# Starting the couples of 64-row products one phase earlier, and a convolution four units later

## The chip, the cores and the metric

The kernel runs on one core of a Trainium2 chip. The metric is device time in microseconds (us). Of this core, five engines matter: TensorE (PE in the profile; its weight loads are listed as PEld), VectorE (DVE), ScalarE (ACT), GpSimd (POOL, almost unused) and SyncE (SP), which issues the transfers. Each engine takes its instructions in the order in which the program wrote them; they wait for each other by semaphores.

## The reference, cut to what matters

```python
# 1. a causal convolution of 7 taps along the sequence; the taps are a softmax, one set per head of 24 channels
w = softmax(weight)                              # 8 heads x 7 taps
x = einsum('hk,bskhg->bshg', w, unfold(pad(x)))  # x: 2 x 4096 x 192
# 2. a feed-forward layer, 192 -> 2048 -> 192
h = x @ w_in
g = where(h >= 1, h, where(h <= -1, 0, (h + 1)**2 / 4))
x = g @ w_out
# 3. a second one with other weights
h = x @ w2_in
out = (h * sigmoid(1.702 * h)) @ w2_out
```

All is in float32. The 8192 tokens are cut into 16 blocks of 512; channels lie on partitions, tokens along the free axis.

## The kernel before, in words

**Units, phases, steps.** The work of one layer on one block is a phase: (1, i) is the first feed-forward layer on block i, (2, i) the second. A phase has 16 units, one for each 128 of the 2048 hidden channels. A list written out by hand sets the order: units 0 to 31 are phases (1, 0) and (1, 1), four units of one and four of the other in turn; units 32 to 47 are (1, 2); 48 to 79 are (2, 0) and (2, 1) in turn; from 80 on, whole phases alternate, (1, 3), (2, 2), (1, 4), (2, 3) and so on to unit 511. Unit numbers serve as steps, too: a plan (`at(step, op)`) says which other work is issued beside which unit.

**One unit.** `gemm1` makes 128 hidden channels of 512 tokens in a PSUM bank `h`. `act_a` applies the activation: for layer 1 a relu and a square on ACT (L272, L273) and a max/min on DVE (L274) that reads `h` again; for layer 2 one gelu on ACT (L276). `act_b` splits the result in two float32r parts: `ghi` by a cast on ACT (L73), `glo` by a subtraction on DVE (L74). `gemm2` multiplies both with the output weights into two accumulator banks; it runs four units (`LAG`) behind `gemm1`. Inputs are split as well: `xah` and `xal` are the parts of a block's first 128 channels, `xb` and `xc` hold the two parts of its 64 last channels.

**Two ways to issue a unit's products.** Up to unit 47 (`WHOLE` = 3 * NF, NF = 16) a unit is ten products over 128 rows, five in `gemm1` and five in `gemm2`. From there on `both(u, v)` issues two units at once: 19 products of `gemm1` u, u+1 and `gemm2` v, v+1 (v = u - 4) that use rows 0 to 63, and 19 that use rows 64 to 127, in turn, so that the two halves of the array run side by side. The lower list begins with `gemm1` and ends with `gemm2`, the upper one the other way round. `act_a` and `act_b` of a couple are issued for both units after it, and behind them the work planned beside its two steps. The first couple, u = `WHOLE`, is still issued with whole products.

**Beside the units** stand three kinds of work. (1) Weights are turned from 64-bit words to two float32r parts in four pieces at steps s to s+3 (`weight_ops`): `begin` (ACT L117, DVE L118), `join` (DVE L122), `high_part` (ACT copy L127, which reads what `join` wrote), `low_part` (DVE L131, L132). For the second layer s = 31 + 9f // 4. (2) `finish` reads an ended phase's accumulators; for layer 1 that is L372, a split into `xah`/`xal`, an add (L374) and a split into `xb`. (3) Convolutions: block 0 and 1 are done at the start; `conv_at(j)` plans those of blocks 2j and 2j+1. For block 2j, seven taps on DVE (L152, L153) make the first 128 channels `cva`, `put_a` splits them into `xah`/`xal`; seven more make the 64 last channels of both blocks `cvb`, and `put_b` splits those. One of these 16 pieces stands at each step from `first - 22` on, where `first` is the unit at which block 2j's phase begins (32 for j = 1, then 112, 176 and so on for j = 2 to 7).

Of the kernel before, what the change touches and what calls it, by code (L numbers as in the profile page):

```python
# [20 lines left out]
def kernel(  # L21
# [24 lines left out]
    NF, _, WC = w1.shape  # L46
    DB = D - P
    B = P // DB
# [1 line left out]
    H = P // 2  # L50
    LAG = 4
    CH = 4
    WHOLE = 3 * NF

    const = ctx.enter_context(tc.tile_pool(name="const", bufs=1))
    wpool = ctx.enter_context(tc.tile_pool(name="wpool", bufs=1))
# [15 lines left out]
    def split(src, hi, lo):  # L72
        nc.scalar.copy(hi, src)  # L73
        nc.vector.tensor_sub(lo, src, f32(hi))  # L74
# [64 lines left out]
    def new_xs():  # L139
        return [xs_p.tile([P, T], F32R, tag=t, name=t) for t in ("xah", "xal", "xb", "xc")]  # L140
# [7 lines left out]
    def conv_taps(part, t, c):  # L148
        def tap(k):
            w, x = taps[:, part, k : k + 1], t[:, k : k + T]  # L150
            if k == 0:
                return lambda: nc.vector.tensor_scalar_mul(c, x, w)  # L152
            return lambda: nc.vector.scalar_tensor_tensor(c, x, w, c, op0=ALU.mult, op1=ALU.add)  # L153

        return [tap(k) for k in range(K)]
# [18 lines left out]
    def put_a(i, c):  # L174
        split(c, *x1[i][:2])

    def swap_halves(dst, src):
        nc.sync.dma_start(f32(dst[0:DB]), f32(src[DB:P]))
        nc.sync.dma_start(f32(dst[DB:P]), f32(src[0:DB]))

    def put_b(i, c):

        b, halved = i % B, phases.index((1, i)) * NF >= WHOLE
        t = x1[i][2 + (b if halved else 0)]
        hi, lo = (t[0:DB], t[DB:P]) if b == 0 else (t[DB:P], t[0:DB])
        split(c[b * DB : (b + 1) * DB], hi, lo)
        if halved:
            swap_halves(x1[i][3 - b], t)

    def conv_ops(j):  # L190

        ta, tb = xt[0, B * j], xt[1, j]
        ca = cv_p.tile([P, T], F32, tag="cva", name="cva")
        cb = cv_p.tile([P, T], F32, tag="cvb", name="cvb", bufs=1)
        x1[B * j] = new_xs()
        ops = conv_taps(0, ta, ca) + [lambda: put_a(B * j, ca)]
        ops += conv_taps(1, tb, cb) + [lambda: put_b(B * j, cb)]
        st = {}

        def begin():  # L200
            st["c"] = cv_p.tile([P, T], F32, tag="cva", name="cva")
            x1[B * j + 1] = new_xs()
            st["ops"] = conv_taps(0, xt[0, B * j + 1], st["c"])
            put_b(B * j + 1, cb)

        ops.append(begin)
        ops += [lambda: st["ops"].pop(0)() for _ in range(K)] + [lambda: put_a(B * j + 1, st["c"])]
        return ops
# [28 lines left out]
    def gemm1(u):  # L237

        ah, al, b, _ = x_of(u)
        h = hid[u] = bank(HID + u % 4, f"h{u}")  # L240
        hi, lo = hidden_w(u)
        prods = [
            (lo[:, 0:P], ah),
            (hi[:, 0:P], al),
            (hi[:, 0:P], ah),
            (lo[:, P : 2 * P], b),
            (hi[:, P : 2 * P], b),
        ]
        for j, (w, r) in enumerate(prods):
            nc.tensor.matmul(h, w, r, start=j == 0, stop=j == len(prods) - 1)  # L250
# [28 lines left out]
    def act_b(u):  # L279
        a = act.pop(u)  # L280
        hi = g_p.tile([P, T], F32R, tag="ghi", name="ghi")
        lo = g_p.tile([P, T], F32R, tag="glo", name="glo")
        split(a, hi, lo)
        halves[u] = (hi, lo)
# [81 lines left out]
    def finish(p, step):  # L366
        n, i = phases[p]
        acc_a, acc_b = accs.pop(p)
        if n == 1:
# [6 lines left out]
            def put():  # L376
                split(s[0:DB], b[0:DB], b[DB:P])
                if phases.index((2, i)) * NF >= WHOLE:
                    swap_halves(c, b)
# [13 lines left out]
    def at(step, op):  # L393
        plan.setdefault(max(step, 0), []).append(op)
# [14 lines left out]
    def fetch_x(*which):  # L409
        for part, i in which:  # L410
            xt[part, i] = x_load(part, i)

    def conv_at(j):
        first, second = (unit_at[phases.index((1, B * j + k)), 0] for k in range(B))
        ops = []
        at(first - 30, lambda: fetch_x((0, B * j), (1, j), (0, B * j + 1)))
        at(first - 22, lambda: ops.extend(conv_ops(j)))
        for k in range(2 * (K + 1)):
            at(first - 22 + k, lambda: ops.pop(0)())
        for k in range(K + 2):  # L420
            at(second - 16 + k, lambda: ops.pop(0)())

    with tc.manual_schedule():
# [14 lines left out]
        ca = cv_p.tile([P, T], F32, tag="cva", name="cva")  # L438
# [31 lines left out]
        for j in range(1, NBLK // B):  # L470
            conv_at(j)
# [5 lines left out]
        def finish_if_last(u, step):  # L477
            if 0 <= u < len(units) and units[u][1] == NF - 1:
                finish(units[u][0], step)


        for step in range(WHOLE):
            gemm1(step)
# [8 lines left out]

        act_b(WHOLE - 1)
        for u in range(WHOLE, len(units) + LAG + 4, 2):
            v = u - LAG
            if u == WHOLE:
                finish_if_last(v - 1, u)
# [71 lines left out]
```

## Time and profile before

| what | us |
|---|---|
| three runs: median (lowest to highest) | 1138.95 (1138.84 to 1139.42) |
| the profiled execution's own time | 1139.2 |
| its span in the trace | 1137.4 |
| PE busy in the span | 1127.7 (99%) |
| ACT busy | 823.3 (72%) |
| DVE busy | 713.7 (63%) |

Busy time is time with at least one instruction of the engine in flight. The products of PE overlap: one lasts about 386 ns, and the next starts 227 ns after it (or at the same time in the other half of the array). So PE's share alone says little; where PE waits, the trace shows it as a gap in brackets with the engine that ended it. Averages over the span also mix the first 130 us, in which all weights are converted, with the rest, in which no weights are.

### The profile page before, as it was taken

How to read it: one execution, taken by the hardware profiler on the slowest of the kernel's cores; microseconds unless marked ns; L12 is line 12 of the kernel's file. 1: busy time of each engine (PE TensorE's matmuls, PEld its weight loads, DVE VectorE, ACT ScalarE, POOL GpSimd, SP SyncE). 2: the span in 40 equal slices, each digit the busy share in tenths (PEclk: the TensorE clock that was granted, in tenths of full speed). 3: DMA queues.
4: the chain of work that ended last, by engine and by line, in shares of the span. 5: the costliest groups of instructions: out<-in, count | busy, mean ns of one | idle time of the engine just before them, and what ended most of it. 6: DMA issues, size and time to landing. Idle time of an engine off the chain costs nothing.

```text
span 1137.4 us, 22818 instructions
## 1 busy us (share of the span) xinstructions
PE 1127.7 (99%) x9324; PEld 927.1 (82%) x9324; DVE 713.7 (63%) x1152; ACT 823.3 (72%) x1467; POOL 7.1 (1%) x13
## 2 busy tenths in 40 slices
PE   9999999999999999999999999999999999999998
PEld 5878888888888888888888888888888888888886
DVE  7998765675557756476564756647566575655432
ACT  7989875867758677686776768677586776868654
POOL 2000000000000000000000000000000000000000
PEclk9999999999999999999999999999999999999999
DMA  5321320100001000010000100010000100000000
GB/s 176 124 65 43 123 75 11 57 10 25 10 11 43 18 17 10 11 43 20 15 20 13 31 20 15 20 43 1 20 15 20 44 1 20 15 20 15 11 15 14
DMA packets 16535, 36.40 MB, mean 32 GB/s; under 512 B 2480, under 2 KB 2480, under 8 KB 16432
## 3 DMA queue, kind: packets, MB, share of 16 engines
q1 hardware_dynamic: 16432, 34.96, 10.5%
q8 instruction: 73, 1.20, 0.5%
q14 instruction: 30, 0.25, 0.1%
HBM read 21.05 MB, written 6.29 MB: 24 GB/s over the span
## 4 chain that ended last, share of the span: by engine, by line
PE 93%; DVE 3%; ACT 2%; issue 1%; DMA 0%; SPq 0%
PE acc L358 46%; PE h L358 42%; PE h L250 3%; DVE glo L74 1%; DVE a L274 1%; PE acc L309 1%; PE acc L312 1%; PE acc L310 1%; PE acc L311 1%; PE ca_ps L170 1%; PE acc L313 1%; DVE wd L122 0%; DVE cva L153 0%; DMA raw<-in_w_dram 0%; ACT a L273 0%
## 5 line engine op out<-in xcount | busy, mean ns | idle before, releaser
L358 PE MATMUL acc<-ghi,wt 64*128 64x512 f32 x2772 | 835.4, 386 | 0.0
L358 PE MATMUL h<-xah,wt 64*128 64x512 f32 x1848 | 714.0, 386 | 0.0
L358 PE MATMUL acc<-glo,wt 64*128 64x512 f32 x1848 | 678.2, 386 | 0.0
L358 PEld LDWEIGHTS acc<-ghi,wt 64*128 64x128 f32 x2772 | 468.9, 184 | 53.9 <-ACT ghi L73 0.3
L74 DVE TENSOR_TENSOR glo<-a,ghi 128x512 fp32r<-128x512 f32 x512 | 341.5, 688 | 232.8 <-ACT ghi L73 223.5
L358 PEld LDWEIGHTS acc<-glo,wt 64*128 64x128 f32 x1848 | 340.4, 184 | 36.5 <-DVE glo L74 0.8
L358 PEld LDWEIGHTS h<-xah,wt 64*128 64x128 f32 x1848 | 340.4, 184 | 36.1 <-issue 0.4
L358 PE MATMUL h<-xal,wt 64*128 64x512 f32 x924 | 357.0, 386 | 0.0
L73 ACT CAST ghi<-a 128x512 fp32r<-128x512 f32 x512 | 301.7, 615 | 26.2 <-DVE a L274 25.7
L274 DVE SCALAR_TENSOR_TENSOR a<-h,a 128x512 f32<-128x512 f32 x256 | 176.9, 691 | 159.7 <-ACT a L273 159.4
L276 ACT ACTIVATE a<-h 128x512 f32<-128x512 f32 x256 | 150.8, 596 | 153.8 <-PE h L358 145.9
L358 PE MATMUL h<-xb,wt 64*128 64x512 f32 x693 | 231.0, 386 | 0.0
L358 PE MATMUL h<-xc,wt 64*128 64x512 f32 x693 | 230.8, 386 | 0.0
L272 ACT ACTIVATE a<-h 128x512 f32<-128x512 f32 x256 | 151.0, 590 | 53.0 <-PE h L358 52.2
L358 PEld LDWEIGHTS h<-xal,wt 64*128 64x128 f32 x924 | 170.2, 184 | 17.8
L273 ACT ACTIVATE a<-a 128x512 f32<-128x512 f32 x256 | 161.8, 632 | 8.2
L358 PEld LDWEIGHTS h<-xc,wt 64*128 64x128 f32 x693 | 127.7, 184 | 17.9
L358 PEld LDWEIGHTS h<-xb,wt 64*128 64x128 f32 x693 | 127.5, 184 | 9.0
L153 DVE SCALAR_TENSOR_TENSOR cva<-xt,taps,cva 128x512 f32<-128x512 f32 x90 | 67.3, 748 | 1.3
L250 PE MATMUL h<-xah,wt 128*128 128x512 f32 x100 | 40.5, 405 | 2.6 <-DVE wt L131 2.6
L153 DVE SCALAR_TENSOR_TENSOR cvb<-xt,taps,cvb 128x512 f32<-128x512 f32 x42 | 31.4, 747 | 0.4
L250 PE MATMUL h<-xb,wt 128*128 128x512 f32 x100 | 30.9, 391 | 0.5 <-DVE xb L74 0.5
(65 smaller groups left out, 488.2 us busy)
## 6 DMA issues: line engine op xcount, KB each, us to landing
raw<-in_w_dram SPq DMA_DIRECT2D x32, 448.0 KB, 3.4
xc<-xb SPq DMA_DIRECT2D x44, 128.0 KB, 2.2
xt<-in_xa_dram SPq DMA_DIRECT2D x16, 259.0 KB, 3.6
out_dram<-o SPq DMA_DIRECT2D x16, 256.0 KB, 2.0
xt<-in_xb_dram SPq DMA_DIRECT2D x8, 259.0 KB, 3.4
out_dram<-o SPq DMA_DIRECT2D x16, 128.0 KB, 2.2
xb<-xc SPq DMA_DIRECT2D x14, 128.0 KB, 2.2
taps<-in_taps_dram SPq DMA_DIRECT2D x1, 7.0 KB, 1.6
```

What stands on the lines that cost most here:

```text
L73: nc.scalar.copy(hi, src)
L74: nc.vector.tensor_sub(lo, src, f32(hi))
L153: return lambda: nc.vector.scalar_tensor_tensor(c, x, w, c, op0=ALU.mult, op1=ALU.add)
L170: return lambda: nc.tensor.matmul(c, d[:, k], t[:, k : k + T], start=k == 0, stop=k == K - 1)
L250: nc.tensor.matmul(h, w, r, start=j == 0, stop=j == len(prods) - 1)
L272: nc.scalar.activation(a, h, AF.Relu, bias=0.5, scale=0.5)
L273: nc.scalar.activation(a, a, AF.Square)
L274: nc.vector.scalar_tensor_tensor(a, h, 1.0, a, op0=ALU.max, op1=ALU.min)
L276: nc.scalar.activation(a, h, AF.Gelu_apprx_sigmoid)
L309: nc.tensor.matmul(acc_a, wl, hi, start=first, stop=False)
L310: nc.tensor.matmul(acc_a, wh, hi, start=False, stop=False)
L358: mm = nc.tensor.matmul(banks[n], w, r, start=n in fresh, stop=ends.get(n) == k)
```

## The change

`WHOLE` becomes 2 * NF: units 34 to 49 (phase (1, 2) but for its first two units, and the two behind it), eight couples, are now issued as 64-row products, and the couple with whole products is 32, 33 instead of 48, 49. As a consequence block 2's 64 last channels are also swapped into `xc` (two more transfers). In `conv_ops` the seven taps and the split of the 64 last channels come ahead of those of the first 128. In `conv_at` these 16 pieces begin at `first - 18`; the pieces of the second block stay at `second - 16`. This holds for every j.

```diff
@@ -50,7 +50,7 @@
     CH = 4
-    WHOLE = 3 * NF
+    WHOLE = 2 * NF
 
@@ -193,8 +193,8 @@
         x1[B * j] = new_xs()
-        ops = conv_taps(0, ta, ca) + [lambda: put_a(B * j, ca)]
-        ops += conv_taps(1, tb, cb) + [lambda: put_b(B * j, cb)]
+        ops = conv_taps(1, tb, cb) + [lambda: put_b(B * j, cb)]
+        ops += conv_taps(0, ta, ca) + [lambda: put_a(B * j, ca)]
         st = {}
@@ -414,9 +414,9 @@
         at(first - 30, lambda: fetch_x((0, B * j), (1, j), (0, B * j + 1)))
-        at(first - 22, lambda: ops.extend(conv_ops(j)))
+        at(first - 18, lambda: ops.extend(conv_ops(j)))
         for k in range(2 * (K + 1)):
-            at(first - 22 + k, lambda: ops.pop(0)())
+            at(first - 18 + k, lambda: ops.pop(0)())
```

On ACT around unit 36 this stood before: casts, the weight copy (L127), the next weights' `begin` (L117) and one unit's activation after the other (`h36` is unit 36's bank; the number after a name tells buffers apart).

```order
L73 CAST ghi_1059<-a_1027 128x512
L127 CAST wt2_89<-wd_1017 128x448
L117 ACTIVATE wa_1069<-raw_994 128x448
L272 ACTIVATE a_1079<-h36_1073 128x512
L273 ACTIVATE a_1079<-a_1079 128x512
L73 CAST ghi_1083<-a_1055 128x512
L372 COPY s_1098<-acc3_1_417 64x512
```

And this stands there now:

```order
L272 ACTIVATE a_1151<-h36_1109 128x512
L273 ACTIVATE a_1151<-a_1151 128x512
L272 ACTIVATE a_1155<-h37_1110 128x512
L273 ACTIVATE a_1155<-a_1155 128x512
L73 CAST ghi_1159<-a_1151 128x512
L73 CAST ghi_1163<-a_1155 128x512
L127 CAST wt2_89<-wd_1104 128x448
L117 ACTIVATE wa_1172<-raw_1096 128x448
L73 CAST xb_1087<-s_1089 64x512
L272 ACTIVATE a_1226<-h38_1182 128x512
```

Both units' casts stand directly ahead of the weight copy, and the next couple's activation stands behind it. On DVE at the same place, before:

```order
L122 SCALAR_TENSOR_TENSOR wd_1017<-wa_1016,wd_1017 128x448
L74 TENSOR_TENSOR xb_987<-s_989,xb_987 64x512
L274 SCALAR_TENSOR_TENSOR a_1055<-h35_1049,a_1055 128x512
L74 TENSOR_TENSOR glo_1060<-a_1027,ghi_1059 128x512
L118 TENSOR_SCALAR wd_1070<-raw_994 128x448
L274 SCALAR_TENSOR_TENSOR a_1079<-h36_1073,a_1079 128x512
```

And now:

```order
L274 SCALAR_TENSOR_TENSOR a_1151<-h36_1109,a_1151 128x512
L274 SCALAR_TENSOR_TENSOR a_1155<-h37_1110,a_1155 128x512
L74 TENSOR_TENSOR glo_1160<-a_1151,ghi_1159 128x512
L74 TENSOR_TENSOR glo_1164<-a_1155,ghi_1163 128x512
L131 TENSOR_TENSOR wt2_89<-wd_1023,wt2_89 128x384
L132 TENSOR_TENSOR wt2_89<-wd_1023,wt2_89 128x64
L122 SCALAR_TENSOR_TENSOR wd_1104<-wa_1103,wd_1104 128x448
```

The `join` (L122) whose result the ACT copy reads stood ahead of unit 35's max/min (copy of `wd_1017`); now it stands behind both subtractions of its couple (copy of `wd_1104`).

On DVE just ahead of unit 112, where block 4 begins, before: the last tap and the split of the 64 last channels, then three couples' subtractions.

```order
L153 SCALAR_TENSOR_TENSOR cvb_2724<-xt_2479,taps_85,cvb_2724 128x512
L74 TENSOR_TENSOR xb_2727<-cvb_2724,xb_2727 64x512
L74 TENSOR_TENSOR glo_3211<-a_3206,ghi_3210 128x512
L74 TENSOR_TENSOR glo_3215<-a_3208,ghi_3214 128x512
L74 TENSOR_TENSOR glo_3267<-a_3262,ghi_3266 128x512
L74 TENSOR_TENSOR glo_3271<-a_3264,ghi_3270 128x512
L74 TENSOR_TENSOR glo_3323<-a_3318,ghi_3322 128x512
L74 TENSOR_TENSOR glo_3327<-a_3320,ghi_3326 128x512
L274 SCALAR_TENSOR_TENSOR a_3374<-h112_3330,a_3374 128x512
```

Now the last tap and the split of the first 128 channels stand one couple's subtractions ahead of it:

```order
L153 SCALAR_TENSOR_TENSOR cva_3019<-xt_2653,taps_85,cva_3019 128x512
L74 TENSOR_TENSOR xal_3022<-cva_3019,xah_3021 128x512
L74 TENSOR_TENSOR glo_3499<-a_3494,ghi_3498 128x512
L74 TENSOR_TENSOR glo_3503<-a_3496,ghi_3502 128x512
L274 SCALAR_TENSOR_TENSOR a_3550<-h112_3506,a_3550 128x512
```

The last of the 16 pieces moved from couple 104 to couple 108, and it is now the split that makes `xah` and `xal`.

## Rows read from the trace of the kernel before

**Rows 1.** Page, part 1: busy us, share of the span, instructions.

```profile
PE 1127.7 (99%) x9324; PEld 927.1 (82%) x9324; DVE 713.7 (63%) x1152; ACT 823.3 (72%) x1467; POOL 7.1 (1%) x13
```

**Rows 2.** Busy us (and instructions) by window; granted clock, DMA share, GB/s.

```profile
50.00:80.00 30.00, 27.37 (x119) 21.85 (x118) 29.95 (x60) 25.47 (x47) 0.00 (x0) 1.00 0.25 77
91.00:127.00 36.00, 36.00 (x161) 29.81 (x160) 31.79 (x62) 34.91 (x66) 0.00 (x0) 1.00 0.34 104
```

**Rows 3.** Timeline of PE, whole products: start, us, instruction, [idle before <-releaser].

```profile
59.07 0.50 PE L250 MATMUL h<-xah,wt 128*128 128x512 f32 x1 [1.03 <-DVE wt L131]
...
75.07 0.39 PE L250 MATMUL h<-xah,wt 128*128 128x512 f32 x1
...
79.25 0.50 PE L250 MATMUL h<-xah,wt 128*128 128x512 f32 x1 [1.60 <-DVE wt L131]
...
90.71 0.39 PE L250 MATMUL h<-xah,wt 128*128 128x512 f32 x1
...
126.98 0.39 PE L250 MATMUL h<-xah,wt 128*128 128x512 f32 x1
```

**Rows 4.** Timeline of DVE, units 10 to 27.

```profile
42.02 0.69 DVE L274 SCALAR_TENSOR_TENSOR a<-h,a 128x512 f32<-128x512 f32 x1 [0.80 <-ACT a L273]
...
46.93 0.69 DVE L274 SCALAR_TENSOR_TENSOR a<-h,a 128x512 f32<-128x512 f32 x1
...
57.26 0.69 DVE L274 SCALAR_TENSOR_TENSOR a<-h,a 128x512 f32<-128x512 f32 x1
...
58.45 0.56 DVE L131 TENSOR_TENSOR wt<-wd,wt 128x384 fp32r<-128x384 f32 x1
...
59.06 0.63 DVE L122 SCALAR_TENSOR_TENSOR wd<-wa,wd 128x448 uint32<-128x448 uint32 x1
...
78.63 0.56 DVE L131 TENSOR_TENSOR wt<-wd,wt 128x384 fp32r<-128x384 f32 x1
```

**Rows 5.** Timeline of ACT, units 10 and 12, then around unit 38.

```profile
40.75 0.58 ACT L272 ACTIVATE a<-h 128x512 f32<-128x512 f32 x1
...
45.47 0.58 ACT L272 ACTIVATE a<-h 128x512 f32<-128x512 f32 x1
...
107.27 0.57 ACT L127 CAST wt<-wd 128x448 fp32r<-128x448 f32 x1 [0.22 <-DVE wd L122]
107.74 0.62 ACT L117 ACTIVATE wa<-raw 128x448 f32<-128x448 f32 x1
108.27 0.57 ACT L272 ACTIVATE a<-h 128x512 f32<-128x512 f32 x1
108.87 0.63 ACT L273 ACTIVATE a<-a 128x512 f32<-128x512 f32 x1
109.41 0.60 ACT L73 CAST ghi<-a 128x512 fp32r<-128x512 f32 x1
109.92 0.62 ACT L73 CAST xb<-s 64x512 fp32r<-64x512 f32 x1
```

**Rows 6.** The first couples of 64-row products: PE at its start, ACT beside.

```profile
131.94 0.39 PE L358 MATMUL h<-xal,wt 64*128 64x512 f32 x1
...
138.04 0.59 ACT L372 COPY s<-acc 64x512 f32<-64x512 f32 x1
...
145.56 0.57 ACT L127 CAST wt<-wd 128x448 fp32r<-128x448 f32 x1 [1.98 <-DVE wd L122]
```

**Rows 7.** PE, ACT and DVE at couple 104, and the start of couple 108.

```profile
248.93 0.39 PE L358 MATMUL h<-xah,wt 64*128 64x512 f32 x1
...
257.54 0.39 PE L358 MATMUL h<-xah,wt 64*128 64x512 f32 x1
...
252.52 0.60 ACT L276 ACTIVATE a<-h 128x512 f32<-128x512 f32 x1 [1.14 <-PE h L358]
...
256.78 0.62 ACT L73 CAST xb<-cvb 64x512 fp32r<-64x512 f32 x1 [1.50 <-DVE cvb L153]
...
257.43 0.69 DVE L74 TENSOR_TENSOR xb<-cvb,xb 64x512 fp32r<-64x512 f32 x1 [0.69 <-ACT xb L73]
```

## The prediction

> **What bounds the kernel now.** I read the busy times first: PE 99% [rows 1], which says only that products are nearly always in flight, so the next view is where PE waits. The timeline of PE has two large gaps, 1.03 us ahead of unit 19 and 1.60 us ahead of unit 27, both ended by the low half of a weight slice from DVE (L131) [rows 3]. Elsewhere a unit of whole products takes (126.98 - 90.71) / 16 = 2.267 us [rows 3], ten products of 0.227 us, and a couple of 64-row products (257.54 - 248.93) / 2 = 4.305 us [rows 7], 19 pairs of 0.227. So after 131 us the span is the couples' count times that, and before it PE is bound except where DVE is late. The windows name the two short stages: between 50 and 80 us DVE is busy 29.95 of 30.00 us, and between 91 and 127 us, where layer 1 of block 2 runs beside the second layer's weights, ACT is busy 34.91 of 36.00 [rows 2]. The change touches both, and one place in the steady part.
>
> **Step 1, fewer products.** A couple costs 20 x 0.227 = 4.53 us whole and 4.305 in halves: 0.227 less for each of the eight couples 34 to 48, -1.8 us. The change between the two ways costs what it did, only earlier: from the start of the whole couple (126.98 [rows 3]) to the first pair of the next (131.94 - 0.23 = 131.71 [rows 6]) it is 4.73 us.
>
> **Step 2, the convolution four units later.** DVE without taps is paced by its exchange with ACT: relu 10 to relu 12 takes 45.47 - 40.75 = 4.72 us [rows 5]. With the short first tap two units take 46.93 - 42.02 = 4.91, and the next four with full taps (57.26 - 46.93) / 2 = 5.16 for two [rows 4]. From unit 10 to unit 16 that was 15.24 us; now units 10 to 13 have no taps and 14, 15 the first two: 4.72 + 4.72 + 4.91 = 14.35, so 0.89 less. From unit 16 to 24 the taps, one split and one short first tap are as many as before. So the slice that unit 27 waits for is written 0.89 us earlier than at 78.63 [rows 4], at 77.74, with its end at 78.3. PE would be there at about 76.4 (75.07 + 2.27 [rows 3], less some 0.9 of the first gap, whose slice also comes 0.89 earlier). It still waits, and unit 32 starts at 90.71 - 0.89 = 89.8 [rows 3]. The rest of the taps now lie in units 25 to 28: DVE needs 1.19 us (57.26 to 58.45 [rows 4]) and a tap of 0.66 per unit, less than the 2.27 of PE, so xal of block 2 is there at about 88.4, ahead of unit 32. Gain 0.9 us; bounds 0 and the two gaps whole, 2.6.
>
> **Step 3, layer 1 in couples beside the weights.** Start to start ACT takes for a relu 0.6, a square 0.54, a cast 0.51, a weight copy 0.47, a weight begin 0.53, a half cast 0.52 [rows 5]. A couple's queue, counted from its first relu: second relu at 1.15, its square ends at 2.4, its max/min on DVE (0.69 [rows 4]) at 3.1, the second cast (0.60) ends at 3.78, its subtraction at 4.50 (hand-overs of 0.04 each included). Only then come on DVE the two weight subtractions (0.61) and the join (0.63) [rows 4], 5.7; the copy on ACT waits for the join, and the begin and the next relu stand behind the copy: next relu at 6.7, or 7.2 with a half cast. That is for couples where join and copy fall together, first steps s odd: slices 0 to 3, copied in couples 32 to 38. The trace has this wait in later couples, 1.98 us ahead of the copy at 145.56 [rows 6], where layer 2 with its single gelu leaves room for it. In couples 40 to 46 the copy finds its join done: 4.2 with a begin alone, 4.67 with copy and begin; still over the 4.305 of PE.
>
> The other side: h of a couple that starts at S is ready at S + 3.59 (252.52 - 248.93 [rows 7]) and, for the second unit, 1.14 later. Couple c+4 multiplies glo of unit c+1 at its sixth pair, 1.13 after its start. So it can't start before relu(c) + 4.50 + 0.05 - 1.13 = relu(c) + 3.42. With whole products the same subtraction had four full units.
>
> The walk: unit 32 at 89.8, couple 34 at 89.8 + 4.73 = 94.5. ACT first does finish of phase 0 (a copy and a cast, 0.6 + 0.5 [rows 6]), so relu 32 is at 92.7 and relu 34 at 92.7 + 6.1 = 98.8 (no weight subtractions yet; h was ready at 98.1). Couple 34 has finish of phase 1 behind its casts, and the join waits for that split too: + 7.77. Then relu 36 at 106.55, relu 38 (+ 7.2) 113.74, relu 40 (+ 6.16, no begin) 119.9, relu 42 (+ 4.2) 124.1, relu 44 128.8, relu 46 133.4. PE is due and can start:
> couple 40: due 107.46, can 109.97, late 2.5;
> couple 42: due 114.4, can 117.2, late 2.8;
> couple 44: due 121.6, can 123.3, late 1.7;
> couple 46: in time at 127.7;
> couple 48: late 0.1; couple 50: late 0.25, at 136.86.
> Each late start adds 0.11 (the first product after a gap lasts 0.50, not 0.39 [rows 3]). Couple 50 starts at 137.0, before at 131.7: +5.3 us with steps 1 and 2 in it, so the waits are 8.0. Behind it layer 2 catches up; it has 0.7 us of backlog at gelu 50 and then the old pattern. The lag of four units hid the whole backlog before; in couples it hides one couple. Bounds: 0, if casts never run late, and 8.0 + 1, if a catch-up of mine fails.
>
> **Step 4, xal one couple before its use.** For j = 2 to 7 the last tap and split move to couple first - 4, into the pattern that the 64 last channels had in couple 104. There the cast on ACT began 7.85 us after the couple's start (256.78 - 248.93) and the split on DVE ended 9.19 after it (257.43 + 0.69) [rows 7]. Couple first starts 8.61 after it and wants xah at once (cast over at 8.47, in time) and xal at its second pair, 8.84: 9.24 less 8.84 is 0.4 late, and 0.11 for the start: 0.5 six times, +3.0 us. Bounds: 0, and 6 x 0.7 if the pattern slips by half a cast. Before, two couples lay between. The order of 64 and 128 channels decides it: xb would be wanted at the fourth pair.
>
> The two more transfers for xc of block 2 are issued by SP around 72 us, while its next transfers, of the second layer's first slices, are 10 us off; couple 34 is the first to read xc. On SP's queue, the swaps behind finish now wait for DVE until 106 and 114; the slices queued behind them are wanted at 123 and later. Both cost nothing; if a swap came 10 us later still, it would delay slice 4 by as much.
>
> **Sum.** -0.9 - 1.8 + 8.0 + 3.0 = +8.3 us on the profiled execution's 1139.2, 1147.5; that execution is 0.25 above the median of 1138.95, so I forecast 1147.2.
>
> The rule that speaks most directly against the change is in the Trainium skill, TensorEngine Tiling (Array Packing), "PSUM Bottleneck": tiling speeds TensorE and not the evacuation of PSUM, which may become the bound; the trace agrees so far as ACT, which does most of that, is at 97% here [rows 2]. By that alone, as throughput, the price is small, as the first rival works out; the order of the queues makes the rest.
>
> **Rivals.** (A) ACT is bound by throughput alone. Its 34.91 us of work in 36 us of whole units [rows 2] would meet 34.2 us of PE in couples (36 x 19 / 20): 0.7 of the 1.8 is not won, and no cast is late beyond that. For it: the trace shows no lateness of ghi or glo in this stage now. Against: the copy's place behind both subtractions, and the 1.98 us wait [rows 6]. 1139.2 - 0.9 - 1.1 + 3.0 - 0.25 = 1140.0, not slower by what counts. It decides if relu 36 starts before 104.0 (107.46 - 3.42) instead of 106.6; with step 4 absent as well it is 1137.0, and with both early gaps gone 1135.3. (B) xal comes in time, as only 0.4 us decide it and any earlier tap removes it: 1147.2 - 3.0 = 1144.2. (C) PE's clock. It stays at 1.00 in every window [rows 2], the one with 1.03 and 1.60 us of gaps included; the new gaps are 2.5 to 2.8 us, longer than any there. If the granted clock fell from 2.4 to 1.2 GHz for one couple, its 4.3 us would double: 1151.5. The Trainium skill, TensorE: Matmul & The Clock Gate, "HAM oscillation", has idle gaps bring the clock down; no gap here has shown it.
>
> **How the numbers follow.** This kernel's measurement can tell about 0.2%, 2.3 us, from no change: 1136.7 to 1141.2 is the same. Forecast 0.66 (own range 1145.4 to 1149.2: 0.2 to 0.7 us for each of step 4's six, and 0.8 more for step 3), B 0.15, C 0.05, A as stated 0.08, A with more gained 0.06. Slower is forecast, B and C, 0.86; the same 0.08; faster 0.06. The range from 1143.2 to 1149.6 holds the forecast and B.
>
> **What would show it.** Right: gaps of PE of 2 to 3 us ahead of the couples 40, 42 and 44, some 107 to 124 us in, ended by ghi or glo; ACT's copy (L127) waiting over 1 us for L122 in couples 34 to 38; DVE's second gap for PE at unit 27 still there and unit 32 0.9 us earlier; a gap of 0.4 us for xal at the start of six phases of layer 1, 32 couples or 137.8 us apart. Wrong: no gap between 100 and 130 us, or relu 36 within 104; the xal gaps missing; a granted clock below 1.00.

## The result, and the profile after

The changed kernel takes 1147.76 us (median of 4 runs, 1146.67 to 1148.95), the kernel before beside it 1139.03: a ratio of 1.0075, 95% interval [1.0063, 1.0086]. Forecast were 1147.2 and slower. The profiled execution took 1146.69 with a span of 1144.9, 7.5 us over the one before. Some runs of these kernels, the one before included, take 2 to 3 us longer than the others, and the two of them that were traced lost it ahead of unit 18 (last section), so parts are compared in the traces from the start of unit 18 on.

The page of the changed kernel, part 1, as in [rows 1]:

```profile
PE 1133.0 (99%) x9468; PEld 923.9 (81%) x9468; DVE 716.0 (63%) x1152; ACT 825.3 (72%) x1467; POOL 6.9 (1%) x13
```

PE's 99% hides the loss: a couple whose products wait between pairs still has products in flight most of the time. The windows of [rows 2], here for the changed kernel, show where it was:

```profile
50.00:80.00 30.00, 28.26 (x123) 22.46 (x122) 29.13 (x58) 26.59 (x50) 0.00 (x0) 1.00 0.28 86
91.00:127.00 36.00, 33.23 (x239) 24.36 (x239) 25.94 (x48) 27.58 (x51) 0.00 (x0) 0.95 0.24 69
```

From 91 to 127 us PE, ACT and DVE all have less busy time than in [rows 2]: 33.23 for 36.00, 27.58 for 34.91, 25.94 for 31.79. ACT was nearly full, and now it waits a quarter of the time while everything runs late. That reads as engines that wait for each other in turn, not as one at its limit; the experiments test it. ACT's queue shows where (timeline of ACT in the changed kernel: relus of units 34, 36, 38, 40, 42, 44 and 46, the weight copies ahead of three of them, and the casts of `xah` for units 112 and 176):

```profile
98.81 0.58 ACT L272 ACTIVATE a<-h 128x512 f32<-128x512 f32 x1
...
105.69 0.57 ACT L127 CAST wt<-wd 128x448 fp32r<-128x448 f32 x1 [1.38 <-DVE wd L122]
...
106.68 0.57 ACT L272 ACTIVATE a<-h 128x512 f32<-128x512 f32 x1
...
112.34 0.56 ACT L127 CAST wt<-wd 128x448 fp32r<-128x448 f32 x1 [1.90 <-DVE wd L122]
...
113.84 0.60 ACT L272 ACTIVATE a<-h 128x512 f32<-128x512 f32 x1
...
119.52 0.57 ACT L127 CAST wt<-wd 128x448 fp32r<-128x448 f32 x1 [1.90 <-DVE wd L122]
119.99 0.59 ACT L272 ACTIVATE a<-h 128x512 f32<-128x512 f32 x1
...
124.20 0.58 ACT L272 ACTIVATE a<-h 128x512 f32<-128x512 f32 x1
...
128.87 0.59 ACT L272 ACTIVATE a<-h 128x512 f32<-128x512 f32 x1
...
133.54 0.58 ACT L272 ACTIVATE a<-h 128x512 f32<-128x512 f32 x1
...
270.63 0.62 ACT L73 CAST xah<-cva 128x512 fp32r<-128x512 f32 x1 [1.50 <-DVE cva L153]
...
408.82 0.62 ACT L73 CAST xah<-cva 128x512 fp32r<-128x512 f32 x1 [1.50 <-DVE cva L153]
```

Each of the three copies waits for the join (L122), and the next relu stands behind the copy. On DVE, in the same couple as the copy at 112.34, the join stands behind both subtractions (and behind two of the weights, 111.08 to 111.77, not shown):

```profile
77.63 0.55 DVE L131 TENSOR_TENSOR wt<-wd,wt 128x384 fp32r<-128x384 f32 x1
...
109.70 1.46 DVE L74 TENSOR_TENSOR glo<-a,ghi 128x512 fp32r<-128x512 f32 x2
...
111.69 0.62 DVE L122 SCALAR_TENSOR_TENSOR wd<-wa,wd 128x448 uint32<-128x448 uint32 x1
...
271.28 0.69 DVE L74 TENSOR_TENSOR xal<-cva,xah 128x512 fp32r<-128x512 f32 x1 [0.69 <-ACT xah L73]
...
409.48 0.69 DVE L74 TENSOR_TENSOR xal<-cva,xah 128x512 fp32r<-128x512 f32 x1 [0.69 <-ACT xah L73]
```

(The first row is the slice for unit 27; the last two are the splits for units 112 and 176.) PE in the changed kernel, at units 18, 19 and 27, the couples 40, 42 and 44, and the couples 112 and 176, where blocks 4 and 6 begin, each with the start of the couple behind it (114 and 178):

```profile
55.39 0.39 PE L250 MATMUL h<-xah,wt 128*128 128x512 f32 x1
...
57.96 0.50 PE L250 MATMUL h<-xah,wt 128*128 128x512 f32 x1
...
78.24 0.50 PE L250 MATMUL h<-xah,wt 128*128 128x512 f32 x1 [1.60 <-DVE wt L131]
...
108.69 0.50 PE L358 MATMUL h<-xah,wt 64*128 64x512 f32 x1 [1.12 <-DVE a L274]
109.62 0.50 PE L358 MATMUL acc<-ghi,wt 64*128 64x512 f32 x1 [0.43 <-ACT ghi L73]
...
116.81 0.49 PE L358 MATMUL acc<-ghi,wt 64*128 64x512 f32 x1 [0.43 <-ACT ghi L73]
...
122.96 0.50 PE L358 MATMUL acc<-ghi,wt 64*128 64x512 f32 x1 [0.43 <-ACT ghi L73]
...
271.39 0.40 PE L358 MATMUL h<-xah,wt 64*128 64x512 f32 x1
271.61 0.39 PE L358 MATMUL acc<-ghi,wt 64*128 64x512 f32 x1
272.03 0.49 PE L358 MATMUL h<-xal,wt 64*128 64x512 f32 x1
...
276.26 0.39 PE L358 MATMUL h<-xah,wt 64*128 64x512 f32 x1
...
409.77 0.39 PE L358 MATMUL h<-xah,wt 64*128 64x512 f32 x1
409.77 0.39 PE L358 MATMUL acc<-ghi,wt 64*128 64x512 f32 x1
410.22 0.49 PE L358 MATMUL h<-xal,wt 64*128 64x512 f32 x1
...
414.46 0.39 PE L358 MATMUL h<-xah,wt 64*128 64x512 f32 x1
```

The two `xal` rows have no bracket, since older products are still in flight, but each was due 0.227 us behind its `xah` row: at 271.62 and 410.00. Such waits are found among the weight loads (the waits of the changed kernel between 140 and 1100 us; columns: engine, line, what it waits for, then us in total, times, longest):

```profile
PEld h L358 <- DVE xal L74: 2.9, 6, 0.5
```

Starts of couples and the end, each counted from unit 18, as the difference to the kernel before (us; minus is earlier; each kernel's profiled execution, the start of unit 18 in the kernel before at 55.61; good to 0.01 or 0.02):

| kernel | unit 32 | couple 50 | couple 110 | end |
|---|---|---|---|---|
| changed | -0.79 | +5.10 | +5.45 | +7.71 |
| convolution alone | -0.76 | -0.75 | -0.76 | +1.53 |
| couples alone | -0.04 | +5.83 | +6.17 | +6.13 |
| changed, blocks 4 on begun as before | -0.78 | +5.16 | +5.49 | +5.45 |
| changed, even slices | -0.81 | +0.62 | +0.97 | +3.22 |
| couples from 40 | -0.78 | -1.45 | -1.45 | -1.49 |
| couples from 36, even slices | -0.81 | -1.29 | -0.90 | -0.94 |
| convolution of block 2 alone | -0.77 | -0.77 | -0.78 | -0.79 |

The changed kernel's 7.71 is thus -0.79 up to unit 32, +5.89 to couple 50, +0.35 to couple 110 and +2.26 over the six phases behind it.

### The profile page after: what moved, and what is told of

Read it like the earlier page. It is cut to its first block, busy times and chain, and to the rows that moved or that the text cites. A ratio compares the mean times of both kernels' runs of the same rounds, so it can differ in the third digit from the quotient of the medians.

```text
span 1144.9 us, 23118 instructions
## 1 busy us (share of the span) xinstructions
PE 1133.0 (99%) x9468; PEld 923.9 (81%) x9468; DVE 716.0 (63%) x1152; ACT 825.3 (72%) x1467; POOL 6.9 (1%) x13
## 4 chain that ended last, share of the span: by engine, by line
PE 91%; DVE 4%; ACT 3%; issue 1%; DMA 0%; SPq 0%; DVEq 0%; ACTq 0%
PE acc L358 46%; PE h L358 41%; PE h L250 2%; DVE glo L74 1%; DVE a L274 1%; DVE cva L153 1%; ACT ghi L73 1%; ACT a L273 1%; ACT a L272 1%; PE ca_ps L170 1%; DVE wd L122 0%; ACT xah L73 0%; DVE xal L74 0%; PE acc L309 0%; PE acc L312 0%
## 5 line engine op out<-in xcount | busy, mean ns | idle before, releaser
L358 PE MATMUL acc<-ghi,wt 64*128 64x512 f32 x2868 | 911.6, 387 | 1.3 <-ACT ghi L73 1.3
L358 PE MATMUL h<-xah,wt 64*128 64x512 f32 x1912 | 739.4, 387 | 1.3 <-DVE a L274 1.3
L358 PE MATMUL acc<-glo,wt 64*128 64x512 f32 x1912 | 734.6, 387 | 0.2
L358 PEld LDWEIGHTS acc<-ghi,wt 64*128 64x128 f32 x2868 | 521.7, 184 | 58.6 <-ACT ghi L73 2.6
L358 PEld LDWEIGHTS acc<-glo,wt 64*128 64x128 f32 x1912 | 352.4, 184 | 41.5 <-DVE glo L74 4.0
L358 PEld LDWEIGHTS h<-xah,wt 64*128 64x128 f32 x1912 | 352.1, 184 | 39.8 <-DVE a L274 2.4
L358 PE MATMUL h<-xal,wt 64*128 64x512 f32 x956 | 370.8, 388 | 0.3
L274 DVE SCALAR_TENSOR_TENSOR a<-h,a 128x512 f32<-128x512 f32 x256 | 176.9, 691 | 179.9 <-ACT a L273 179.8
L358 PE MATMUL h<-xb,wt 64*128 64x512 f32 x717 | 240.1, 388 | 0.0
L127 ACT CAST wt<-wd 128x448 fp32r<-128x448 f32 x32 | 18.1, 567 | 21.5 <-DVE wd L122 21.5
L250 PE MATMUL h<-xah,wt 128*128 128x512 f32 x68 | 28.0, 412 | 1.8 <-DVE wt L131 1.6
```

The source lines that it names most:

```text
L127: nc.scalar.copy(w[:, 0:WC], f32(st["d"]))
L274: nc.vector.scalar_tensor_tensor(a, h, 1.0, a, op0=ALU.max, op1=ALU.min)
L358: mm = nc.tensor.matmul(banks[n], w, r, start=n in fresh, stop=ends.get(n) == k)
```

## The experiments

**The two halves of the change by themselves.** Theory 1 is the prediction's: late casts in the couples and late `xal` are two separate costs. First the convolution's order and start alone:

```diff
-    WHOLE = 2 * NF
+    WHOLE = 3 * NF
```

> The convolution's later place and new order alone (couples begin at unit 48, as before). Theory 1 (the forecast's steps): DVE writes the weight slice for unit 27 some 0.8 us earlier, and xal comes late for the six blocks j = 2 to 7, 0.34 us each as the changed kernel's trace has it, 2.1 together: 1139.0 - 0.8 + 2.1 = 1140.3, six gaps of PE for xal, no gap between 85 and 145 us, granted clock 1.00 throughout. Rival: the move costs nothing by itself (the xal gaps need the couples' backlog), then 1138.2.

It took 1140.8 us (median of 11 runs, 1140.12 to 1142.28) beside 1139.14 for the kernel before (15 runs, for the next three experiments, too): ratio 1.0013 [1.0004, 1.0022]; theory 1 had 1140.3, the rival 1138.2. The wait of the changed kernel for `xal` is here again, to the tenth: 2.9 us in 6 waits, the longest 0.5.

The table gives -0.75 at couple 50 and +1.53 at the end, so six waits cost 2.28 us, 0.38 each on average, where the prediction had 0.5 each.

Then the couples alone (against the kernel before):

```diff
-    WHOLE = 3 * NF
+    WHOLE = 2 * NF
```

> The couples from unit 32 alone; the convolution as before. Theory 1: the eight couples give 1.8 us and ACT's late casts cost 8.0: 1139.0 + 6.2 = 1145.2, gaps of PE of 1 to 2.5 us ahead of couples 40, 42, 44, as much as 2.2 more in runs whose clock falls at a second gap; no xal gap. Rival: the late casts come from the convolution's last pieces at units 25 to 29, which push ACT and DVE into the couples; then the gaps are gone or under 1 us here, and the time is 1137.2 to 1139.

It took 1145.95 us (5 runs, 1144.8 to 1148.48), ratio 1.0061 [1.0049, 1.0074]; theory 1 had 1145.2, the rival 1139 at most. PE is idle ahead of the couples 40, 42 and 44 for 1.11, 1.18 and 0.17 us and for 0.43 behind the first product of each, where gaps of 1 to 2.5 us were expected. So the couples cost four fifths of it, the convolution's move the rest, and the two add up: +1.53 and +6.13 make 7.66, with 7.71 measured in one kernel.

**Moving `xal` back.** In the changed kernel, blocks 4 to 15 get their early start again, with the 64 last channels still first:

```diff
-        ops = []
+        ops, lead = [], 18 if j == 1 else 22
-        at(first - 18, lambda: ops.extend(conv_ops(j)))
+        at(first - lead, lambda: ops.extend(conv_ops(j)))
...
-            at(first - 18 + k, lambda: ops.pop(0)())
+            at(first - lead + k, lambda: ops.pop(0)())
```

> The changed kernel, with the 16 pieces beginning at first - 18 for j = 1 alone and at first - 22 for the others (64 last channels still first). Theory 1: xal is split two couples ahead again, no gap at the start of blocks 4, 6, ... 14, 2.1 us less than the changed kernel: 1144.6 where that one takes 1146.7, 1146.8 where it takes 1148.9. Rival: the gap moves to the next late piece (xb or the swap), and the time stays within 0.5 us of the changed kernel's.

It took 1144.97 us (5 runs, 1144.32 to 1147.14), ratio 1.0054 [1.0041, 1.0067]. Behind couple 50 nothing waits for `xal` any more, and the end comes 7.71 - 5.45 = 2.26 us earlier, with 2.1 expected. So without the late start the order costs nothing. Whether the late start would cost anything with the old order, in which `xb` comes last, was not run.

**Taking the copy away from behind the subtractions.** The mechanism of step 3 stands and falls with join and copy in one couple, which the odd steps of slices 0 to 3 bring about. In the changed kernel these four begin at even steps:

```diff
+            s += s % 2 if f < 4 else 0
```

> The changed kernel with the four pieces of the second layer's weight slices 0 to 3 beginning at steps 32, 34, 36, 38 instead of 31, 33, 35, 37, so that the join falls in the couple ahead of its copy. The same work on ACT and DVE. Theory 1 (the copy that waits for the join holds up the next relu): relu 36 near 104.4 us, 38 near 110.3, 40 near 115.0, then 4.67 us each; gaps of 0.3 us or less but for 1.6 ahead of couple 42 (the half cast there waits for the add behind both subtractions); couple 50 starts 4.4 us earlier than in the changed kernel, 1142.3, and no fall of the clock. Rival (ACT bound by its busy time alone): nothing changes, 1146.7 to 1148.9.

It took 1144.46 us (5 runs, 1142.06 to 1145.45), ratio 1.0039 [1.0026, 1.0052]. Two of the runs took 1142.06 and 1142.32, as expected; the other three took over 2 us more, and the profiled one, which is of these, lost it ahead of unit 18. Counted from unit 18, its trace ends 3.22 us later than the kernel before, which would make 1142.3, and couple 50 starts 4.48 us earlier than in the changed kernel, with 4.4 expected. In its ACT timeline the relus of units 36, 38, 40 and 42 and the copies of two couples:

```profile
105.68 0.57 ACT L127 CAST wt<-wd 128x448 fp32r<-128x448 f32 x1
...
107.18 0.59 ACT L272 ACTIVATE a<-h 128x512 f32<-128x512 f32 x1
...
111.01 0.56 ACT L127 CAST wt<-wd 128x448 fp32r<-128x448 f32 x1
...
113.30 0.59 ACT L272 ACTIVATE a<-h 128x512 f32<-128x512 f32 x1
...
117.96 0.58 ACT L272 ACTIVATE a<-h 128x512 f32<-128x512 f32 x1
...
122.62 0.58 ACT L272 ACTIVATE a<-h 128x512 f32<-128x512 f32 x1
```

Unit 18 starts 2.93 us later in this trace than in the changed kernel's (58.32 for 55.39); less that, the relus of units 36, 38 and 40 are at 104.25, 110.37 and 115.03, where 104.4, 110.3 and 115.0 were expected. The copies wait for nothing, and a couple with copy and begin takes ACT 122.62 - 117.96 = 4.66 us, the prediction's 4.67. That is still over PE's 4.305. The 1.6 us expected ahead of couple 42 came spread over two couples: 40 and 42 take 5.04 and 5.58 us. Moving four slices by one step thus gives back 4.48 of the 5.89 us lost up to couple 50 with the same work on both engines; that part is the order. What is left, +1.43 us where the pairs alone should have given -1.8, is consistent with ACT's 4.66 a couple and the half cast that waits.

**Couples that start behind the first four slices.** If that is the cause, couples may begin at unit 40, with the convolution of block 2 alone moved (`halved` says whether block 2 needs `xc`):

```diff
-    WHOLE = 2 * NF
+    WHOLE = 40
-        b, halved = i % B, phases.index((1, i)) * NF >= WHOLE
+        b, halved = i % B, (phases.index((1, i)) + 1) * NF > WHOLE
-        ops = []
+        ops, lead = [], 18 if j == 1 else 22
```

(and `lead` in place of 18, as above)

> Couples begin at unit 40 instead of 32 (the first one whole, so halves from 42), the convolution begins four units later for block 2 only and keeps its 64 last channels first. Theory: the lateness of the changed kernel comes from the first four slices of the second layer's weights, whose copy on ACT stands behind both subtractions of a couple; here these four fall beside whole units, so no product waits for ghi, glo or an h bank between 95 and 130 us. What is left are the four couples 42 to 48 in halves (4 x 0.227 = 0.9 us less) and the earlier unit 32 (0.8 us less), with no wait for xal at the six phases: 1139.1 - 1.7 = 1137.4 us, 0.9985 of the kernel before. Rival: ACT is at its limit over the whole second layer's weights, so couples there cost a few us wherever they begin: 1139 us or more.

It took 1137.87 us (11 runs, 1137.36 to 1139.59) beside 1139.27 for the kernel before (27 runs): ratio 0.9988 [0.998, 0.9997]. Waits between 95 and 137 us, and the window from 91 to 127:

```profile
PEld acc L358 <- DVE glo L74: 0.3, 2, 0.2
...
ACT wt L127 <- DVE wd L122: 0.2, 1, 0.2
```

```profile
91.00:127.00 36.00, 36.00 (x221) 30.42 (x221) 31.67 (x60) 33.71 (x63) 0.00 (x0) 1.00 0.31 92
```

PE is full again, and the copies' wait for the join has shrunk from the changed kernel's 6.5 us (four waits between 95 and 137 us) to 0.2. The theory holds (1137.4 expected), the rival's 1139 or more does not: where the first four slices are not among them, couples beside the second layer's weights keep 0.67 of the 0.9 us that they should save (-1.45 at couple 50, -0.78 at unit 32). This version beats the kernel before by 1.4 us.

**The same from unit 36, with even slices.** As the last, with `WHOLE = 36` and the line of the even slices:

> Couples begin at unit 36 (first one whole, halves from 38), slices 0 to 3 of the second layer's weights are begun at even steps so that their copy needn't wait behind a couple's subtractions; convolution as in the kernel with couples from 40. Theory: six couples in halves save 1.36 us and the convolution 0.8, but a couple with copy and begin occupies ACT for 4.67 us against PE's 4.31, so each of some three couples comes about 0.3 late: 1137.5 to 1138.5 us. Rival: the backlog of the whole units before (a lag of four units) takes up the 0.36 us per couple and nothing is late: 1136.9 us.

It took 1138.17 us (11 runs, 1137.94 to 1140.15), ratio 0.9995 [0.9986, 1.0003], inside the theory's range. Its waits between 95 and 137 us name one operand:

```profile
PEld acc L358 <- DVE glo L74: 2.0, 7, 0.4
```

Up to couple 44 nothing is late; then the couples 44, 46 and 48 take 4.39, 4.57 and 4.68 us instead of 4.305. So the whole units' backlog takes up ACT's excess for three couples, and then PE goes at the pace of ACT's queue, 4.67. Of the 1.36 and 0.8 us 1.29 are left at couple 50, and 0.94 at the end.

**The convolution of block 2 alone.** Couples from 48 as before, `lead` as above:

> The couples begin at unit 48 as in the kernel before; the convolution begins four units later for block 2 only (j = 1), and its 64 last channels come first for every j. Theory: only unit 27's earlier slice is left: 1139.1 - 0.8 = 1138.3 us, no wait for xal at the six phases. Rival: the later start is worth nothing by itself (the 0.8 us that unit 32 is earlier are taken back in the first layer's remaining units or at the first couple): 1139.1 us.

It took 1138.56 us (11 runs, 1137.93 to 1141.21), ratio 0.9997 [0.9988, 1.0006]: the times can't tell it from no change. The trace can (PE at units 19 and 27):

```profile
57.71 0.50 PE L250 MATMUL h<-xah,wt 128*128 128x512 f32 x1 [0.16 <-DVE wt L131]
...
77.99 0.50 PE L250 MATMUL h<-xah,wt 128*128 128x512 f32 x1 [1.60 <-DVE wt L131]
```

The gap of 1.03 us ahead of unit 19 [rows 3] is down to 0.16, the one ahead of unit 27 is whole, and the 0.77 us gained by unit 32 are still there at the end (-0.79).

**The changed kernel once more.**

> The changed kernel itself, to see its runs beside the ones of this call. Theory: its runs fall in two groups, about 1146.7 and 1149.0 us, by what happens ahead of unit 18 (first weight transfer later, granted clock lower between 15 and 21 us), and the part behind unit 18 is the same in both: 1086.4 less to more by under 0.3 us from unit 18 to the end, that is 7.7 us longer than in the kernel before. Rival: the upper group loses its time behind unit 18, at the couples 40 to 44, where the granted clock fell in one profile: then its distance from unit 18 to the end is over 1 us longer.

It took 1146.78 us (5 runs, 1146.54 to 1147.25), ratio 1.0066 [1.0052, 1.008]. All five lie in the lower group, so it does not show the upper one. From unit 18 to the end its trace has 1089.56 us, 7.75 more than before and 0.04 more than the changed kernel's first trace (1089.52; the expectation's 1086.4 fits neither); the granted clock fell in both.

## Why the prediction was right

The direction and the size hold: 8.3 us on the profiled execution were forecast, 7.5 measured, 7.71 from unit 18 on. The median of 1147.76 stands so near to 1147.2 partly by chance, since two of its four runs are 2.2 us above the other two; of all nine runs of the changed kernel seven lie between 1146.54 and 1147.25. Two of the prediction's signs did not come as written: PE has no single gaps of 2 to 3 us ahead of the couples 40, 42 and 44, since the wait is split within the couples (see step 3), and the granted clock went below 1.00, which stood among the signs of being wrong.

**Step 1 and the switch** are as worked out: no couple shows another count of products (38), and where nothing waits (couples from 40) four couples and the switch gave 1.45 - 0.78 = 0.67 us of the forecast 0.9.

**Step 2** forecast 0.9 us by unit 32; it is 0.79 in the changed kernel and 0.76 and 0.77 where the convolution was moved without the couples. The slice for unit 27 is written at 77.63, forecast 77.74, and PE still waits 1.60 us for it, as in [rows 3]: the first gap went, the second one moved.

**Step 3** held in its working. The walk had the relus 34 to 46 at 98.8, 106.55, 113.74, 119.9, 124.1, 128.8 and 133.4; the rows above have 98.81, 106.68, 113.84, 119.99, 124.20, 128.87 and 133.54. From unit 32 to couple 50 it forecast +6.2 us (5.3 and 0.9); measured are +5.89, and 0.35 more up to couple 110, which it had taken to be caught up. Rival A, ACT bound by throughput alone, fell with relu 36 at 106.68 (its bound was 104.0) and with the even slices, which leave ACT the same work and give 4.48 us back. Two details were not in it: the first product of couple 40 waits for the bank of `h`, which unit 36's max/min still reads (1.12 us, L274), and the second pair for `ghi`, not yet `glo`. So the couples start earlier than the walk had them, 40 and 42 at 108.69 and 115.87 instead of 109.97 and 117.2, and lose the rest inside. The last wait of the couple is the walk's: `glo` of the second unit can't be used before relu + 4.55, which is 118.39 for couple 42 and 124.54 for couple 44, and the weight loads of its first product there start at these times:

```profile
118.40 0.18 PEld L358 LDWEIGHTS acc<-glo,wt 64*128 64x128 f32 x1 [0.26 <-DVE glo L74]
...
124.55 0.18 PEld L358 LDWEIGHTS acc<-glo,wt 64*128 64x128 f32 x1 [0.24 <-DVE glo L74]
```

(In couple 40 the lower clock, below, took the place of this last wait; in the kernel with the couples alone it is there as well.)

**Step 4** is the term that was mis-sized, 3.0 us forecast and 2.26 measured. It took 0.4 us of lateness and 0.11 for the start from couple 104's rows [rows 7]. At couple 112 that is what happened, to the hundredth: the cast begins 270.63 - 262.78 = 7.85 us after couple 108, the split ends 9.19 after it, and `xal` is multiplied at 272.03, 0.41 late. But this first wait changes the pattern. Ahead of it the lower list runs one product ahead of the upper one (`xah` at 271.39, the upper list's `ghi` at 271.61); behind it the two go in step (both at 409.77), so a couple's first product comes one product later against all that follows it. At couple 176 the cast begins 408.82 - 401.16 = 7.66 after couple 172, and `xal` is 0.22 late. The rows of the couples behind show the price: 276.26 - 271.39 = 4.87 us for couple 112, 0.56 over the 4.305, and 414.46 - 409.77 = 4.69 for couple 176, 0.38 over. With 0.38 to 0.40 for each of the other four that is 2.5 us, and about 0.22 comes back because the upper list, which was one product behind, no longer is: 2.26 at the end. The prediction's 0.5 was near for the first phase, and it carried that over to all six. Rival B (`xal` in time) fell by the six waits.

**Rival C**, a lower granted clock, came, from about 110.2 to 113.6 us, and cost nothing that the table shows; the section on the hardware has its rows. Its price, 4.3 us, assumed that PE was what the couple waited for, and there ACT and DVE were.

## What to carry to other kernels

When two units' work is issued together, look at what else falls into the same couple on the engines that exchange results: a copy behind a join behind two subtractions made a ring of two engines of 7.2 us where PE needs 4.3, though both engines then stood idle a quarter of the time. Walk such a queue in program order with durations from the trace, and look whether moving a piece by one step cures it before taking work away: here that gave 4.48 of 5.89 us back. And a saving of 0.2 us per couple is soon eaten by one operand that comes a fraction of a microsecond late in each phase: here two couples between the last split and its first product were enough, and one was not.

## What the runs showed of the hardware

**The granted clock fell, and not always.** Windows of the changed kernel:

```profile
110.00:112.00 2.00, 1.97 (x12) 1.26 (x10) 1.91 (x5) 0.44 (x1) 0.00 (x0) 0.54 0.15 61
112.00:114.00 2.00, 2.00 (x14) 1.57 (x12) 1.22 (x4) 1.66 (x4) 0.00 (x0) 0.61 0.00 0
```

After PE had been idle for 1.12 and 0.43 us with a single product between, the clock went to 1.2 GHz from about 110.2 to 113.6 us, and pairs came 0.43 us apart instead of 0.227. The same kernel in its second trace had it, too, after gaps of 1.11 and 0.43 us:

```profile
110.00:112.00 2.00, 1.77 (x12) 1.05 (x14) 1.91 (x4) 0.71 (x2) 0.00 (x0) 0.98 0.42 158
112.00:114.00 2.00, 2.00 (x12) 1.53 (x12) 1.72 (x5) 1.15 (x3) 0.00 (x0) 0.50 0.00 0
```

So had the kernel with blocks 4 on begun as before (gaps of 1.13 and 0.43 us, clock 0.53 between 114 and 116 us). The kernel with the couples alone had the same two gaps (1.11 and 0.43 us) and kept 2.4 GHz:

```profile
110.00:112.00 2.00, 1.34 (x7) 0.59 (x8) 1.46 (x4) 1.64 (x3) 0.00 (x0) 1.00 0.80 257
112.00:114.00 2.00, 2.00 (x18) 1.49 (x20) 2.00 (x5) 0.21 (x1) 0.00 (x0) 1.00 0.00 0
```

Yet from unit 32 to couple 50 it lost 5.83 + 0.04 = 5.87 us, and the changed kernel 5.10 + 0.79 = 5.89: slower products only filled a wait for ACT and DVE. In the kernel with the couples alone PE, at full clock, was idle for another 1.18 us ahead of couple 42, and in the changed kernel it was not. The Trainium skill, TensorE: Matmul & The Clock Gate, "What's actually happening", says that the point at which the clock changes at a kernel's start differs from run to run of one kernel. The traces show the like for the fall: in the two of the changed kernel it came about 1.5 and 2.7 us after the first gap's end (0.54 and 0.98 between 110 and 112 us, with the gap ended at 108.69 and 109.21). Whether that is why it stayed away in the kernel with the couples alone is not shown, as that kernel was traced once. The gap ahead of unit 27, 1.60 us in each of the ten traces, never brought it down.

**A late first transfer can cost twice.** In the trace of the kernel with blocks 4 on as before, DVE's first weight instruction and the window from 15 to 18 us:

```profile
7.62 0.39 DVE L118 TENSOR_SCALAR wd<-raw 128x448 uint32<-128x448 uint32 x1 [1.55 <-DMA raw<-in_w_dram]
```

```profile
15.00:18.00 3.00, 3.00 (x7) 1.72 (x6) 1.80 (x6) 1.86 (x4) 0.00 (x0) 0.52 0.51 152
```

and the same in the changed kernel:

```profile
6.51 0.50 DVE L118 TENSOR_SCALAR wd<-raw 128x448 uint32<-128x448 uint32 x1 [0.56 <-DMA raw<-in_w_dram]
```

```profile
15.00:18.00 3.00, 3.00 (x10) 1.64 (x9) 1.81 (x5) 2.91 (x6) 0.00 (x0) 1.00 0.50 153
```

The transfer came 1.1 us later, all that hangs on it followed, and between 15 and 18 us the clock was at or near 1.2 GHz. Ahead of that PE had been idle for 0.95, 0.35 and 0.52 us between its first products, in the changed kernel for 0.36 and 0.53. The trace with the even slices shows the same (DVE waits for 1.80 us, clock 0.51), and unit 18 starts at 58.1 and 58.3 us in these two, in the others between 55.1 and 56.1. The changed kernel's second trace has the transfer 0.6 us later than its first, the clock at 1.00, and unit 18 just 0.5 us later: there the delay cost only once. Only two of the longer runs were traced; that the others are of the same kind, and why they were more frequent with some kernels (3 of 5 with the even slices, 1 of 11 with the convolution alone), stays open.
